# A one-row output stored as four pieces from two queues, in a decode kernel with grouped attention and two MLP steps

## The chip, the cores and the metric

The kernel runs on 1 core of one Trainium2 chip. The metric is device time in microseconds (us), the median of several runs. Beside it stands one profiled execution, whose trace gives the start and duration of every instruction. The engines are TensorE (PE; its weight loads PEld), VectorE (DVE), ScalarE (ACT), GpSimd (POOL) and SyncE (SP). A name with a q (SPq, ACTq) is the engine's instruction queue, which also issues transfers (DMAs).

## What is computed

One token of 512 numbers goes through a layer norm, an attention over a cache of 16,384 positions with 32 query heads on 8 key/value heads, and a second block. With a sequence of one, all four shifted groups of that block are zero, so that only its layer norm and the two-layer MLP are left.

```
x = A_x                                                   # (1, 1, 512) bf16
h = x + _A_ref(_layernorm(x), A_k_cache, A_v_cache, A_wq, A_wo)
h2 = h + _B_ref(_layernorm(h), B_w1, B_w2, B_w3, B_w4)
...
def _A_ref(x, k_cache, v_cache, wq, wo):
    q = heads(x @ wq)
    scores = einsum("bhqd,bhkd->bhqk", q, repeat(k)) * Dh ** -0.5
    o = einsum("bhqk,bhkd->bhqd", softmax(scores), repeat(v))
    return merge(o) @ wo
def _B_ref(x, w1, w2, w3, w4):
    hs = concatenate(shifted groups of gelu(layernorm(x) @ w1)) @ w2
    x1 = x + hs
    return x1 + gelu(layernorm(x1) @ w3) @ w4
```

The output is one row of 512 bf16 numbers, 1 KB.

## The kernel before

The caches and weights, some 79 MB, are streamed from device memory by SyncE through the helper `load` (its DMA is L216). For each of the 8 key/value heads, VectorE transposes the keys (`kt`, L390), TensorE makes scores (L399), ScalarE exponentiates (L425), TensorE transposes the weights and multiplies by the values (L455), and the results are gathered (L467). Keys are held in a ring of two buffers `kb`, values in a ring of three `vb`; the last loads are the output projection `wo` and the MLP weights w3 and w4, w4 in four pieces. ScalarE issues a single load, the input `x4` (four rows of 128 numbers), at the start.

The end of the program goes: the projection with `wo` (L533), the row's mean and variance, the product with w3 (L546), gelu on ScalarE (L558), a transpose on VectorE (L562), the product with w4 (L567), and the sum on VectorE into `fin` (L571). `fin` is a tile of 128 partitions by 128 numbers. TensorE worked with each column copied 32 times, so partitions 0, 32, 64 and 96 hold the four quarters of the output and the other partitions hold copies. The store (L573) takes these four partitions, 256 B each, and writes them to the four quarters of `out`.

The order on each engine is that in which the code records the operations: `Program.op` keeps a list per engine, works out which earlier operations each one depends on, and `emit` turns these into semaphore waits ahead of the instruction. Every DMA has a semaphore of its own name, which is raised by 16 when the whole transfer has landed. The last operation, a `nop` on SyncE that reads the output, makes SyncE wait for the landing; in the built program that wait stands on the branch that leaves the block (L146). Behind it come a drain on each engine and a barrier over all of them, and the program ends.

Of the kernel before, what the change touches and what calls it, by code (L numbers as in the profile page):

```python
# [131 lines left out]
def bass_sequential_preLN__gqa_block_cached__mixer_s_mlp__decode_kernel(  # L132
# [13 lines left out]
    with ExitStack() as ctx:  # L146
        sb = lambda name, shape, dt: ctx.enter_context(nc.sbuf_tensor(name, shape, dt))
        ps = lambda name, shape, dt: ctx.enter_context(nc.psum_tensor(name, shape, dt))
        P = Program(nc, ctx)
# [49 lines left out]
        fin = sb("fin", [128, 128], BF16)  # L199
# [48 lines left out]
        def piece(cuts, m):  # L248
            return [lo <= m < hi for lo, hi in cuts].index(True)
# [71 lines left out]
        for b in range(2):  # L321
            for e_ in range(2):
                n = 2 * b + e_
                P.op("POOL", lambda e, n=n, b=b, e_=e_: e.affine_select(
                    out=selq_f[:, n, :], in_=selq_f[:, n, :], pattern=[[-2, 32]], compare_op=ALU.not_equal,
# [5 lines left out]
            r=["ident"], w=["quarter"])  # L331
# [8 lines left out]
            r=["hT", (("st", 0), 0), (("st", 0), 6)], w=["xn"])  # L340
# [3 lines left out]
            r=["selq_f"], w=["selq"])  # L344
        dve(lambda e: e.memset(nscale[:, :], -SCALE), w=["nscale"])
        act(lambda e: e.activation(scr[0:1, 0:1], mean4[0:1, 0:1], ACTF.Exp), r=["mean4"], w=["scr"])
        for i in range(2):
# [5 lines left out]
            r=["ident_f"], w=["row32"])  # L353
        dve(lambda e: e.tensor_reduce(row4[:, :], row32[:, :].rearrange("p (a u h) -> p u h a", a=4, u=2)[:, 0, :, :], AX.X, ALU.add),
            r=["row32"], w=["row4"])
        dve(lambda e: e.tensor_reduce(maskdd[:, :], ident_f[:, :].rearrange("p (n d) -> p d n", d=4), AX.X, ALU.add),
            r=["ident_f"], w=["maskdd"])
# [3 lines left out]
            r=["row32"], w=["zo"])  # L361
# [4 lines left out]
        for h in range(HQ):  # L366
            for k in range(NCH):
# [3 lines left out]
                   r=["xn"] + [("wo", n) for n in range(len(WO))], w=["n"], bank=["mn"])  # L371
# [100 lines left out]
        for g in range(HKV + 1):  # L472
# [33 lines left out]
            if g == HKV - 1:  # L506
# [7 lines left out]
                for n, (lo, hi) in enumerate(W4):  # L514
                    load(f"w4{n}", w4_sb[:, lo:hi, :], w4_in[:, lo:hi, :], ("k", 1, 2 + n))
                act(lambda e: e.activation(scr[0:1, 1:2], mean4[0:1, 0:1], ACTF.Gelu_apprx_tanh),
                    r=["mean4"], w=["scr"])
# [8 lines left out]
            r=["o_m"], w=["o_f"])  # L526
# [3 lines left out]
           r=["quarter", "x4"], w=[("O", 0)], bank=[("O", 0)])  # L530
        for r_ in range(32):
            for q in range(4):
# [3 lines left out]
                   r=["o_b", ("wo", piece(WO, r_))], w=[("O", 0)], bank=[("O", 0)])  # L536
# [4 lines left out]
            r=["hT", (S, 0)], w=["hc"])  # L541


        for k in range(NCH):
            for q in range(4):
                pe(lambda e, k=k, q=q: e.matmul(s_ps[32 * q:32 * q + 32, 0, 0:FQ], hc[:, k, :],  # L546
                                                w3_sb[:, k, q * FQ:(q + 1) * FQ], start=(k == 0), stop=(k == NCH - 1)),
                   r=["hc", ("k", 1, piece(W3, k))], w=[("s", 0)], bank=[("s", 0)])
# [5 lines left out]
            r=["hr", (S, 0), (S, 6)], w=["xs"])  # L554
# [10 lines left out]
        for m in range(NHC):  # L565
            for o in range(4):
# [3 lines left out]
                   r=[("hcol", 2 * m // NHC), ("k", 1, 2 + piece(W4, m))], w=["n"], bank=["mn"])  # L570
        dve(lambda e: e.tensor_tensor(fin[:, :], xsum[:, :], n_ps[:, 0:128], ALU.add),  # L571
            r=["n", "xsum"], w=["fin"], bank=["mn"])
        P.op("SP", lambda e: e.dma_start(out[0, 0:1, :].rearrange("o (q j) -> (o q) j", q=4), fin[0:128:32, :]),  # L573
             r=["fin"], w=["out"], dma="out")
        P.op("SP", lambda e: e.nop(), r=["out"])
        P.emit()

    return nc
# [28 lines left out]
```

## Time and profile before

| | us |
|---|---|
| median of 3 runs | 193.95 (193.80 to 193.97) |
| the profiled execution | 194.09 |
| its span, first to last instruction | 192.3 |
| VectorE busy in it | 120.1 |
| TensorE busy in it | 112.8 |
| ScalarE busy in it | 16.9 |

The DMA engines move 79.32 MB at a mean of 413 GB/s, and their busy share is nine tenths or more in 38 of the 40 slices of the span; the first slice has six tenths and the last one. The profiled execution's time is 1.8 us longer than its span: what lies before the first and behind the last recorded instruction.

Times in the views are in us from the span's start unless marked ns. A row of the timeline has the start, the duration, the engine, the line, the operation and its tiles; an x and a number say how many instructions were merged. A DMA's row on a queue is the time for which the engine was occupied with issuing it, not the transfer. In the list of waits a row names who waited, for whom, the total, how often and the longest. In the listing of one line's instructions, the three numbers are the shortest, median and longest duration in ns.

### The profile page before, as it was taken

What the parts mean: (1) busy time and instruction counts of PE and PEld (TensorE: products, weight loads), DVE (VectorE), ACT (ScalarE), POOL (GpSimd) and SP (SyncE); (2) the same over time, 40 slices, a digit from 0 to 9 for tenths busy, and PEclk for the clock granted to TensorE, in tenths of its full rate; (3) what the DMA queues carried; (4) which work ended last, traced back from release to release, by engine and by line L of the source; (5) the groups of instructions that cost most, each with busy time, mean ns of one, the idle gap of its engine ahead of it and who ended that gap; (6) DMA issues with size and microseconds to landing.
All of it is one profiled execution on the core that took longest, in us unless ns stands there. A gap on an engine that the chain in (4) does not pass through costs nothing.

```text
span 192.3 us, 2626 instructions
## 1 busy us (share of the span) xinstructions
PE 112.8 (59%) x1106; PEld 55.9 (29%) x1106; DVE 120.1 (62%) x225; ACT 16.9 (9%) x38; POOL 6.6 (3%) x26
## 2 busy tenths in 40 slices
PE   1025045658837766774686558645785676595443
PEld 1025001242234235223422432233223422454311
DVE  4844099499349929964795369546953796303170
ACT  3000000030030030003000300030003000600010
POOL 2000000000000000000000000000000000000060
PEclk9999999999985695588559655975558559669555
DMA  6999999999999999999999999999999999999991
GB/s 232 436 429 429 433 436 426 436 441 433 406 426 464 429 392 426 477 433 392 423 447 419 429 416 433 443 433 416 447 445 412 402 429 423 426 418 421 417 376 48
DMA packets 5066, 79.32 MB, mean 413 GB/s; under 512 B 576, under 2 KB 576, under 8 KB 1344
## 3 DMA queue, kind: packets, MB, share of 16 engines
q1 hardware_dynamic: 5048, 79.17, 96.9%
q8 instruction: 8, 0.13, 0.3%
q14 instruction: 2, 0.02, 0.0%
q10 hardware_dynamic: 8, 0.00, 0.0%
HBM read 79.17 MB, written 0.00 MB: 412 GB/s over the span
## 4 chain that ended last, share of the span: by engine, by line
DMA 40%; DVE 14%; SPq 5%; issue 2%; PE 1%
DMA kb<-in_A_k_cache_dram 30%; DVE kt L390 13%; DMA kb<-in_B_w_dram 10%; SPq L216 5%; DVE mx L407 1%; PE T_ps L435 0%; DVE pt L441 0%; PE mn_ps L567 0%; DVE fin L571 0%; PE A_ps L446 0%; SPq L102 0%; DVE o_sb L464 0%
## 5 line engine op out<-in xcount | busy, mean ns | idle before, releaser
L390 DVE STREAM_TRANSPOSE kt<-kb 128x1024 int32<-128x1024 int32 x64 | 74.0, 1212 | 11.2 <-DMA kb<-in_A_k_cache_dram 11.1
L399 PE MATMUL s_ps<-kt,qb 128*32 128x512 bf16 x256 | 47.5, 556 | 32.3 <-DVE kt L390 32.3
L455 PE MATMUL O_ps<-vb,pt 128*16 128x512 bf16 x224 | 28.9, 529 | 0.0
L399 PEld LDWEIGHTS s_ps<-kt,qb 128*32 128x32 bf16 x256 | 10.6, 113 | 61.9 <-DVE kt L390 54.1
L425 ACT ACTIVATE p_sb<-s_ps,bias 128x512 bf16<-128x512 f32 x16 | 12.8, 824 | 150.1 <-PE mn_ps L419 114.1
L467 PE MATMUL A_ps<-o_sb,zo 128*128 128x128 f32 x64 | 15.7, 422 | 10.3 <-DVE o_sb L464 10.3
L441 DVE COPY pt<-T_ps 64x256 bf16<-64x256 bf16 (+2 forms) x40 | 9.8, 261 | 15.6 <-PE T_ps L435 15.2
L407 DVE TENSOR_REDUCE mx<-s_ps 128x1 f32<-128x512 f32 x16 | 10.8, 677 | 11.9 <-PE s_ps L399 9.9
L435 PE MATMUL T_ps<-ident,p_sb 128*128 128x128 bf16 x128 | 11.8, 250 | 10.9 <-ACT p_sb L425 10.9
L467 PEld LDWEIGHTS A_ps<-o_sb,zo 128*128 128x128 f32 x64 | 13.4, 310 | 11.4 <-DVE o_sb L464 11.4
L435 PEld LDWEIGHTS T_ps<-ident,p_sb 128*128 128x128 bf16 x128 | 8.9, 112 | 12.9 <-ACT p_sb L425 12.7
L455 PEld LDWEIGHTS O_ps<-vb,pt 128*16 128x16 bf16 x224 | 9.4, 114 | 9.8 <-issue 8.5
L368 PE MATMUL mn_ps<-xn,wqo 128*128 128x1 bf16 x128 | 3.6, 165 | 9.1 <-DMA wqo<-in_A_wq_dram 9.1
L412 PE MATMUL mn_ps<-ident_f,mx 128*1 128x128 f32 x32 | 7.3, 323 | 2.5 <-DVE mx L407 2.5
L464 DVE COPY o_sb<-O_ps 128x512 f32<-128x512 f32 x8 | 5.5, 691 | 4.9 <-PE O_ps L455 4.6
L431 POOL COPY p_sb<-p_sb 128x64 bf16<-128x64 bf16 x8 | 1.9, 236 | 160.7 <-ACT p_sb L425 160.7
L368 PEld LDWEIGHTS mn_ps<-xn,wqo 128*128 128x128 bf16 x128 | 3.5, 104 | 9.2 <-issue 9.2
L415 DVE TENSOR_REDUCE nm<-mn_ps 1x4 f32<-1x256 f32 x8 | 3.2, 406 | 3.7 <-PE mn_ps L412 3.7
L533 PE MATMUL O_ps<-wqo,o_b 128*32 128x128 bf16 x128 | 3.0, 253 | 3.0 <-DMA wqo<-in_A_wo_dram 1.7
L412 PEld LDWEIGHTS mn_ps<-ident_f,mx 128*1 128x1 f32 x32 | 2.3, 90 | 7.7 <-DVE mx L407 5.4
L419 PEld LDWEIGHTS mn_ps<-nm,nscale 1*128 1x128 f32 x16 | 2.5, 198 | 5.5 <-DVE nm L415 5.5
L258 DVE TENSOR_SCALAR_CACHE_REDUCE hr<-O_ps 128x128 f32<-128x128 f32 x2 | 0.6, 292 | 5.5 <-PE O_ps L533 4.8
(79 smaller groups left out, 55.9 us busy)
## 6 DMA issues: line engine op xcount, KB each, us to landing
kb<-in_A_k_cache_dram SPq DMA_DIRECT2D x8, 4096.0 KB, 26.7
vb<-in_A_v_cache_dram SPq DMA_DIRECT2D x14, 2048.0 KB, 24.4
wqo<-in_A_wq_dram SPq DMA_DIRECT2D x1, 4096.0 KB, 12.4
kb<-in_A_v_cache_dram SPq DMA_DIRECT2D x2, 2048.0 KB, 26.6
wqo<-in_A_wo_dram SPq DMA_DIRECT2D x2, 1280.0 KB, 32.8
kb<-in_B_w_dram SPq DMA_DIRECT2D x1, 1344.0 KB, 22.9
wqo<-in_A_wo_dram SPq DMA_DIRECT2D x1, 1024.0 KB, 36.2
kb<-in_B_w_dram SPq DMA_DIRECT2D x1, 640.0 KB, 24.8
```

The lines of the kernel that those rows point to most:

```text
L216: P.op(by, lambda e: e.dma_start(dst, src), w=[key, *also], dma=name)
L368: pe(lambda e, h=h, k=k: e.matmul(n_ps[:, h:h + 1], wqo[:, k * HQ * DH + h * DH:k * HQ * DH + (h + 1) * DH], xn[:, k:k + 1], start=(k == 0 ...
L390: dve(lambda e, i=i, view=view: e.transpose(view(kt), view(kb[i])), r=[("k", i, n) for n in range(KPARTS)], w=[("kt", t)])
L399: pe(lambda e, g=g, half=half, n=n, ct=ct, c8=c8: e.matmul(s_ps[32 * ct:32 * ct + 32, half, :], qb[:, n, g, :, :, :].rearrange("p a u h -> ...
L407: dve(lambda e: e.tensor_reduce(mx[:, half:half + 1], s_ps[:, half, :], AX.X, ALU.max), r=[("s", half)], w=[("mx", half)], bank=[("s", half)])
L412: pe(lambda e, half=half: e.matmul(m_ps[0:1, half * 128:half * 128 + 128], mx[:, half:half + 1], ident_f[:, :], start=True, stop=True), r= ...
L425: act(lambda e, half=half, g=g: e.activation(p_sb[:, half * 512:half * 512 + 512].rearrange("p (l s x) -> p l x s", l=8, x=2), s_ps[:, hal ...
L435: pe(lambda e, w=w: e.transpose(T_ps[:, w, :], p_sb[:, w * 64:w * 64 + 128], ident[:, :]), r=[("p", w // 8), ("p", (w + 1) // 8), "ident"] ...
L441: dve(lambda e, lo=lo, w0=w0, w1=w1, l0=l0: e.tensor_copy(to[lo:lo + 64, l0:l0 + w1 - w0, :, :], of[lo:lo + 64, w0:w1, :, lo // 64, 0, :]) ...
L455: pe(lambda e, q=q, ct=ct, n=n: e.matmul(O_ps[g % 2][32 * ct:32 * ct + 16, :], pt[g % 2][:, ct, A, 4 * q:4 * q + 4, :].rearrange("p l h -> ...
L464: dve(lambda e, g=g: e.tensor_copy(o_sb[g % 2][:, :], O_ps[g % 2][:, :]), r=[("O", g % 2)], w=[("osb", g % 2)], bank=[("O", g % 2)])
L467: pe(lambda e, g=g, j=j: e.matmul(A_ps[:, 0:128], zo[:, j, 112 - 16 * g:240 - 16 * g], o_sb[g % 2][:, j * 128:(j + 1) * 128], start=False, ...
```

## The change

The one store of four rows on SyncE becomes four stores of one row each: quarters 0 and 2 are issued by SyncE, 1 and 3 by ScalarE. Each has a semaphore of its own (`out0` to `out3`), and the last operation on SyncE waits for all four. The instruction order of TensorE, VectorE and GpSimd is unchanged.

```
-        P.op("SP", lambda e: e.dma_start(out[0, 0:1, :].rearrange("o (q j) -> (o q) j", q=4), fin[0:128:32, :]),
-             r=["fin"], w=["out"], dma="out")
-        P.op("SP", lambda e: e.nop(), r=["out"])
+        for q in range(4):
+            P.op(("SP", "ACT")[q % 2], lambda e, q=q: e.dma_start(out[0, 0:1, q * 128:(q + 1) * 128],
+                                                                  fin[32 * q:32 * q + 1, :]),
+                 r=["fin"], w=[("out", q)], dma=f"out{q}")
+        P.op("SP", lambda e: e.nop(), r=[("out", q) for q in range(4)])
```

## The prediction

> **What bounds the kernel now.** I read the chain of waits first, cut to its last 32 us. The columns are start, duration, what:
>
> ```profile
> 169.90 0.04 issue
> 169.94 19.49 DMA kb<-in_B_w_dram
> 189.43 0.04 issue
> 189.48 0.43 PE mn_ps L567 x5
> 189.91 0.02 issue
> 189.94 0.29 DVE fin L571
> ```
>
> The kernel streams weights and caches until 189.43 us: the last piece of w4 lands, the last matmuls of L567 run for 0.43 us, and VectorE writes `fin` in 0.29 us. The chain view stops there, but the program does not. What follows comes from the timeline of the last microseconds, then from the waits of SyncE's queue, then from the listing of the instructions of L146 (the end of the block):
>
> ```profile
> 190.25 0.63 SPq L573 DMA_DIRECT2D out_dram<-fin  x1
> ```
>
> ```profile
> SPq L146 <- DMA out_dram<-fin: 1.0, 1, 1.0
> ```
>
> ```profile
> L146 SPq COMPARE_BRANCH x1: 33/33/33, 191.9 to 191.9; - x1
> L146 SPq DRAIN x1: 7/7/7, 192.1 to 192.1; - x1
> ```
>
> So the store sits naked at the end. It is issued for 0.63 us (190.25 to 190.88), SyncE waits 1.0 us more for the landing (about 191.9), then branches, drains and passes the closing barrier until the span ends at 192.3. Nothing else runs: the other engines stand in that barrier. A microsecond added before the landing is a microsecond of span. The change touches only this stretch.
>
> **The change, part by part.** It removes one issue on SyncE of 0.63 us. It adds two issues on SyncE, one behind the other, and two on ScalarE, one behind the other, all four released by the same `fin`. SyncE then waits for four semaphores, not one. Nothing is moved past other work: behind each queue stands only the closing barrier, and the order of PE, DVE and POOL is the same.
>
> *What one issue costs* is not in the trace for a single-row store, so I bound it by the rows for other issues. The listing of L216 (the helper `load`) gives minimum, median and maximum in ns, and the chain gives the pattern inside one batch of loads:
>
> ```profile
> L216 SPq DMA_DIRECT2D vb<-in_A_v_cache_dram x14: 327/328/531, 2.1 to 140.0; - x14
> L216 ACTq DMA_DIRECT2D x<-in_A_x_dram x1: 553/553/553, 0.7 to 0.7; - x1
> L216 SPq DMA_DIRECT2D wqo<-in_A_wq_dram x1: 391/391/391, 0.7 to 0.7; - x1
> ```
>
> ```profile
> 160.93 0.33 SPq L216
> 161.26 0.04 issue
> 161.30 0.43 SPq L216
> 161.73 0.04 issue
> ```
>
> A load of 128 rows takes SyncE 0.33 us when it comes alone and 0.43 us right behind another, with 0.04 us between. The only store takes 0.63 us. ScalarE has one issue in the whole trace: `x4`, 4 rows of 256 B, 0.55 us.
>
> On SyncE, two issues therefore take between 0.33 + 0.04 + 0.43 = 0.80 us (priced as loads) and 0.63 + 0.04 + 0.63 = 1.30 us (priced as the store), or 1.40 us if the second pays the 0.10 us that loads pay back to back. Against 0.63 us this is +0.17 to +0.77.
>
> On ScalarE the nearest row is `x4`: same engine, rows of the same size. Two of these take 0.55 + 0.04 + 0.55 = 1.14 us, or +0.51 against 0.63 us. The low bound is the load price on SyncE (+0.17); the high one is 0.63 + 0.04 + 0.73 = 1.40 us, or +0.77.
>
> The two engines work side by side, so the later pair counts. By their nearest rows that is ScalarE's, unless SyncE's pair is priced wholly as the store. I take +0.51. What it is covered by: nothing, since `fin` is the last computation. ScalarE itself is free in time: its last activation (L558) starts at 185.93 and takes 0.85 us for its two pieces.
>
> *From the end of an issue to the landing* I keep the 1.0 us of the old store for each new one. It cancels. Its bounds: four landings at once could be slower by what I can't price except by queueing (below); a smaller one could be quicker. The windows view (window, length, busy time of five engines, clock, DMA share, GB/s) shows when bytes moved, for the store and for the first loads:
>
> ```profile
> 191.20:191.40 0.20, 0.00 (x0) 0.00 (x0) 0.00 (x0) 0.00 (x0) 0.00 (x0) 0.50 0.00 0
> 191.40:191.60 0.20, 0.00 (x0) 0.00 (x0) 0.00 (x0) 0.00 (x0) 0.00 (x0) 0.50 0.03 5
> ```
>
> ```profile
> 1.40:1.60 0.20, 0.00 (x0) 0.00 (x0) 0.00 (x0) 0.20 (x1) 0.20 (x1) 1.00 0.00 0
> 1.60:1.80 0.20, 0.00 (x0) 0.00 (x0) 0.11 (x1) 0.20 (x1) 0.20 (x2) 1.00 3.05 823
> ```
>
> The store's bytes move in 191.4 to 191.6, at least 0.52 us after its issue ended at 190.88. After the `x4` issue, which ended at 1.26, the first bytes come in 1.6 to 1.8, as early as 0.34 us. So a new store could gain about 0.2 us here (0.52 - 0.34 = 0.18): the low bound of this term is -0.2, the high one 0.
>
> The Trainium skill, in DMA: Bandwidth & Descriptors, section "Latency and other measured facts", puts most of the fixed cost of a small DMA into the receipt of the write at its target. By that rule four stores in flight would share one receipt and the extra issues would hardly matter (the second rival, below). The trace agrees in part only: of 1.65 us from issue to landing at least 1.15 us are over before the first byte moves, and at most 0.5 us (191.4 to 191.9) is left for the receipt.
>
> *The waits.* In the changed program SyncE waits first for `out3` (ScalarE's second), then in one instruction for `out1` and `out2`, and the closing branch waits for `out0`. Before, the branch alone waited. A wait that is already satisfied has this price in the listing of L102:
>
> ```profile
> L102 SPq EVENT_SEMAPHORE x19: 17/17/17, 33.8 to 160.9; - x19
> ```
>
> With about 0.03 us of issue beside it (as in the chain at 160.90) that is 0.05 us each. `out3` lands last by the sum above, so the two steps behind it lie on the path: +0.10. If SyncE's store were last, one step follows: +0.05.
>
> *Sum:* +0.51 + 0.10 = +0.61 us. Bounds: the low one is the load price, quicker first bytes and one wait, 0.17 - 0.2 + 0.05 = about 0; the high one without queueing between the engines is 0.77 + 0.10 = +0.87. The profiled execution took 194.09 us (span 192.3, the rest around it, which the change does not touch), so it would become 194.70. The median of the runs shown is 193.95, 0.14 us less; the same step gives 194.56, which I forecast.
>
> **The rivals.** The bound between same and different is 0.2%, 0.39 us, about what a measurement of this kernel tells from no change: faster is below 193.56, slower above 194.34.
>
> 1. *All single rows issue like loads, on both engines.* Then the pair costs +0.17 and the waits +0.10: +0.27, 194.22, within the bound. For it: 0.33 us is the commonest price on SyncE, and the store's 0.63 may come from its step over four partitions 32 apart, which a single row lacks. Against it: ScalarE's only issue shows 0.55, and it is a plain load.
>
> 2. *Not slower: a store of one row starts its bytes sooner, by what the second issue costs.* Load prices (+0.17), first bytes 0.2 us sooner after the issue, as after `x4` (-0.2), and one wait (+0.05): +0.02, 193.97. It decides when the time from the end of the second issue to the landing falls below 1.0 - 0.17 - 0.05 = 0.78 us. For it: the 0.34 us to first bytes after `x4`. Against it: `x4` is a load from another engine, and its window holds the bytes of `wq` too. A gain above 0.39 us would need the old 0.63 us issue to shrink more than two new ones add, and no row shows an issue under 0.327 us, so two exceed it.
>
> 3. *The two engines queue for one another.* If the four issues run in series, the last ends after 4 x 0.43 + 3 x 0.04 = 1.84 us, +1.21, and with one wait +1.26: 195.21. Priced as the store they would take 4 x 0.63 + 0.12 = 2.64 us, +2.01 and 196.0. Against it speaks the start of the span: ScalarE's `x4` and SyncE's `wq` are issued together (0.71 and 0.72 us), and `wq` takes 0.39 us, only 0.06 above the 0.33 alone. For it: `x4` itself took 0.55, and how much of that was waiting can't be seen. The Trainium skill, in Perfetto Trace Analysis, section "DMA Instruction — HWDGE (DVE, Sync)", says that the block that generates descriptors is locked by one issuer at a time, and that the wait for the lock is counted in the instruction's duration. By that rule full series would give the 195.21 above; the 0.06 us of `wq` shows little of it here.
>
> **How the numbers follow.** The forecast has 0.54: each step has a row of the right engine or kind. Rival 1 has 0.17, since it needs a price on ScalarE that no row shows. Rival 2 has 0.10, needing two favourable bounds together. Rival 3 has 0.16: one overlap speaks against it, but four issues in a microsecond were never seen. The remaining 0.03 is a drift of the whole program below 193.56 with no mechanism. Slower: 0.52 of the forecast (0.02 is for its lower edge under 194.34) and 0.16, together 0.68. Same: 0.17 + 0.02 and 0.08 of rival 2, 0.27. Faster: 0.02 of rival 2 by drift and 0.03, 0.05. The range runs from 194.0 (rival 2's time, half of it left out) to 195.2 (rival 3 with load prices; the part above it left out). The forecast's own range is 194.3 (+0.51 - 0.2 + 0.05) to 194.8 (+0.87).
>
> **What would show it.** In the changed profile the two SPq rows and the two ACTq rows should start near 190.25. If ScalarE's rows are 0.55 us or more and end after SyncE's, and SyncE's longest wait at the end names ScalarE's second store, the forecast's path is right. Rows of 0.33 and 0.43 on both engines mean rival 1 or 2; the window in which the last bytes move then decides: bytes less than 0.4 us after the last issue mean rival 2. Rows on one engine that grow while the other's run, to a sum above 1.4 us, mean rival 3. The distance from the last landing to the span's end is 0.4 us now and should be 0.1 more. The packets also tell how a row is cut: the page counts 576 packets under 512 B, and 35 loads of 16 small packets plus 8 each for `x4` and the store make 576. With one data packet a row it stays 576. The prediction is wrong if the stretch before 190.25 changes by more than the forecast itself, or if the last issue ends before 191.05.

## The result and the profile after

The changed kernel takes 194.29 us in the median of 20 runs (194.09 to 194.68), the kernel before 194.04 in 20 runs beside it (193.80 to 194.27). The ratio is 1.0015, with a 95% interval of 1.0009 to 1.0021; by the medians it is 0.25 us slower. That is a loss clear of the noise, but inside the bound of 0.2% that the prediction called the same. The forecast was +0.61 us.

The end of the timeline after the change (start, duration, engine, line, operation, tiles, number merged):

```profile
190.02 0.29 DVE L571 TENSOR_TENSOR fin<-xsum,mn_ps 128x128 bf16<-128x128 f32 x1 [2.10 <-PE mn_ps L567]
190.34 0.62 SPq L574 DMA_DIRECT2D out_dram<-fin  x2
190.34 0.55 ACTq L574 DMA_DIRECT2D out_dram<-fin  x2
```

Two single-row stores take SyncE 0.62 us and ScalarE 0.55 us, where the one store of four rows took 0.63. The listing of L574 separates them (shortest, median, longest, in ns):

```profile
L574 SPq DMA_DIRECT2D out_dram<-fin x2: 254/288/323, 190.3 to 190.7; - x2
L574 ACTq DMA_DIRECT2D out_dram<-fin x2: 248/259/270, 190.3 to 190.6; - x2
```

A single row is issued in 0.25 to 0.32 us. In the trace the second row is the shorter one on SyncE (0.25 after 0.32) and 0.02 us longer on ScalarE (0.27 after 0.25). The bytes move in two groups (windows view: window, length, five engines, clock, DMA share, GB/s):

```profile
191.00:191.10 0.10, 0.00 (x0) 0.00 (x0) 0.00 (x0) 0.00 (x0) 0.00 (x0) 0.50 0.03 5
191.10:191.30 0.20, 0.00 (x0) 0.00 (x0) 0.00 (x0) 0.00 (x0) 0.00 (x0) 0.50 0.00 0
191.30:191.40 0.10, 0.00 (x0) 0.00 (x0) 0.00 (x0) 0.00 (x0) 0.00 (x0) 0.50 0.02 3
191.40:191.50 0.10, 0.00 (x0) 0.00 (x0) 0.00 (x0) 0.00 (x0) 0.00 (x0) 0.50 0.01 3
```

The first stores' bytes go in 191.0 to 191.1, the second stores' in 191.3 to 191.5. Measured from the end of `fin` (190.31 here, 190.22 before), the last bytes leave within 1.2 us, and before the change they left at 1.2 to 1.4. Then come the waits, in the list of SyncE's queue and the listings of L577 (the closing `nop`) and L146:

```profile
SPq L102 <- DMA out_dram<-fin: 0.8, 1, 0.8
```

```profile
L577 SPq EVENT_SEMAPHORE  x1: 130/130/130, 191.8 to 191.8; - x1
```

```profile
L146 SPq COMPARE_BRANCH  x1: 33/33/33, 192.0 to 192.0; - x1
```

SyncE waits 0.8 us for `out3`, then 0.13 us more in the wait for `out1` and `out2`: its own second store lands last, not ScalarE's. From the end of `fin` to the start of the closing branch, to the nanosecond in the trace, it takes 1.71 us, against 1.68 before. The part of the program that the change touches became 0.03 us longer.

So where do 0.25 us come from? Each run has both its device time and its span. Their difference, the time around the span, shows where they lie: it is 1.80 us on average in the 29 runs of the kernel before that were taken beside the first experiments (1.75 to 1.87) and 2.03 in the 20 runs of the changed one (1.92 to 2.09). The spans of single runs are on record to 0.1 us, so the averages are what counts. The mean span is 192.24 before and 192.28 after. Most of the loss lies outside the recorded instructions, where the prediction had put nothing. The page still counts 576 packets under 512 B, so each row went as one data packet. The experiments look for what moved the time around the span, and for what an issue's price hangs on.

The table holds what they gave. "ScalarE" is the number of instructions more than in the kernel before (built program, without waits). "Tail" is the time from the end of `fin` to the start of SyncE's closing branch in the profiled execution. "Around" is the mean over the runs of device time minus span. Times are medians, the kernel before in its own batch beside them. All in us.

| kernel | ScalarE | tail | around | time | before |
|---|---|---|---|---|---|
| before | 0 | 1.68 | 1.80 | | 194.04 |
| changed | +2 | 1.71 | 2.03 | 194.29 | 194.04 |
| e1_one_sem | +2 | 1.65 | 2.00 | 194.15 | 194.05 |
| e2_all_sp | 0 | 2.18 | 1.80 | 194.56 | 194.05 |
| e3_four_act | +1 | 1.70 | 1.81 | 193.94 | 194.05 |
| e4_adjacent | 0 | 1.22 | 1.80 | 193.60 | 194.05 |
| e5_two_acts | +2 | 1.67 | 2.02 | 194.14 | 194.05 |
| e6_all_act | +4 | 2.16 | 2.00 | 194.57 | 194.05 |
| e7_pairs | +1 | 1.31 | 1.81 | 193.68 | 194.05 |
| e8_x4_three | +2 | 1.67 | 2.02 | 194.25 | 194.05 |
| e9_after_one_gelu | +1 | 1.72 | 1.82 | 194.03 | 193.98 |
| e10_before_one_gelu | -1 | 1.67 | 1.81 | 194.00 | 193.98 |
| e11_pairs_one_sem | +1 | 1.32 | 1.80 | 193.68 | 193.98 |
| e12_step2 | 0 | 1.77 | 1.81 | 194.10 | 193.98 |

### The profile page after: what moved, and what is told of

Same layout as the page of the kernel before. It is cut to its first block, busy times and chain, and to the rows that moved or that the text cites. A ratio compares the mean times of both kernels' runs of the same rounds, so it can differ in the third digit from the quotient of the medians.

```text
span 192.4 us, 2631 instructions
## 1 busy us (share of the span) xinstructions
PE 112.3 (58%) x1106; PEld 56.2 (29%) x1106; DVE 120.1 (62%) x225; ACT 16.9 (9%) x38; POOL 6.6 (3%) x26
## 4 chain that ended last, share of the span: by engine, by line
DMA 40%; DVE 14%; SPq 5%; issue 2%; PE 1%
DMA kb<-in_A_k_cache_dram 30%; DVE kt L390 13%; DMA kb<-in_B_w_dram 10%; SPq L216 5%; DVE mx L407 1%; PE T_ps L435 0%; DVE pt L441 0%; PE mn_ps L567 0%; DVE fin L571 0%; DVE o_sb L464 0%; PE A_ps L446 0%; SPq L102 0%
## 5 line engine op out<-in xcount | busy, mean ns | idle before, releaser
L455 PE MATMUL O_ps<-vb,pt 128*16 128x512 bf16 x224 | 28.3, 516 | 0.0
L533 PE MATMUL O_ps<-wqo,o_b 128*32 128x128 bf16 x128 | 3.5, 305 | 1.3 <-DVE o_b L527 1.3
L419 PE MATMUL mn_ps<-nm,nscale 1*128 1x4 f32 x16 | 3.2, 270 | 1.3 <-DVE nm L415 0.9
```

The lines of the kernel that those rows point to most:

```text
L419: pe(lambda e: e.matmul(n_ps[:, 0:REP], nscale[0:1, :], nm[0:1, :], start=True, stop=True), r=["nm", "nscale"], w=["n"], bank=["mn"])
L455: pe(lambda e, q=q, ct=ct, n=n: e.matmul(O_ps[g % 2][32 * ct:32 * ct + 16, :], pt[g % 2][:, ct, A, 4 * q:4 * q + 4, :].rearrange("p l h -> ...
```

## The experiments

**One semaphore (e1).** The changed kernel, with the four stores raising one semaphore:

```
-                 r=["fin"], w=[("out", q)], dma=f"out{q}")
+                 r=["fin"], w=[("out", q)], dma="out")
```

> The changed kernel with one semaphore for the four stores, so that the closing branch alone waits (for 64). Theory A (the small loss lies at the end of the program: the last landing plus the two extra wait steps): the two SPq and two ACTq rows stay at 0.62 and 0.55 us in sum, the stretch from the last store row's end to the branch shrinks by about 0.07 us, and the time falls from +0.25 to about +0.15 to +0.2 us against the kernel before. Theory B (the loss hangs on the number of semaphores or on what lies outside the span): the time returns to within 0.05 us of the kernel before. Theory C (the loss hangs on ScalarE issuing at the end): the time stays at +0.25 us.

Measured: 194.15 against 194.05, ratio 1.0009 (1.0000 to 1.0018). The tail shrinks by 0.06 us to 1.65, less than before the change: three semaphores more cost the two extra steps behind the last landing and, as far as these runs show, nothing else. The time around the span stays at 2.00. So theory B falls in its first half (the number of semaphores), and what is left of the loss is neither the landings nor the waits.

**All four on one engine (e2, e6).** The changed kernel with one name in place of the alternation:

```
-            P.op(("SP", "ACT")[q % 2], lambda e, q=q: e.dma_start(out[0, 0:1, q * 128:(q + 1) * 128],
+            P.op("SP", lambda e, q=q: e.dma_start(out[0, 0:1, q * 128:(q + 1) * 128],
```

and "ACT" in place of "SP" in e6.

> All four single rows issued by SyncE, with four semaphores. Theory A: rows of 0.25 to 0.32 us with 0.04 between make about 1.2 us of issue in place of 0.63, so the time is 0.5 to 0.6 us above the kernel before. Theory C (ScalarE at the end costs 0.2 us by itself): only 0.3 to 0.4 us above. If single rows were issued at the price of the old store (0.63 us each), it would be about 2.0 us above.

> All four single rows issued by ScalarE. Inside the span, from the end of fin to SyncE's closing branch, about 2.15 to 2.2 us as with all four on SyncE (2.18), 0.5 more than before. Theory E (the 0.2 us outside the span come with the number of DMAs that ScalarE issues, three or more, its load included): time minus span 2.0 and time about 0.7 us above the kernel before. Theory F (they come when both queues carry the output's stores): time minus span 1.80 and time 0.5 us above.

Measured: 194.56 with SyncE alone, ratio 1.0026 (1.0016 to 1.0036); 194.57 with ScalarE alone, 1.0032 (1.0020 to 1.0044). Both tails are about 0.5 us longer than before, as reckoned from rows of 0.25 us. The listings of L574 in e2 and in e6:

```profile
L574 SPq DMA_DIRECT2D out_dram<-fin x4: 246/254/312, 190.3 to 191.3; - x4
```

```profile
L574 ACTq DMA_DIRECT2D out_dram<-fin x4: 240/274/275, 190.1 to 191.0; - x4
```

Alone on its engine a row is issued in the same time as beside the other engine's rows, so the two engines don't queue for one another in issuing. The time around the span is 1.80 with SyncE alone, which issues three DMAs more and waits twice more than before, and 2.00 with ScalarE alone. Theory F (both queues at once) falls with that. The time of e6 fits less well: tail and time around the span add up to +0.68 us, and its six runs give +0.52 by the medians and +0.62 by the ratio.

**The four-row store on ScalarE (e3).** The kernel before, one name changed:

```
-        P.op("SP", lambda e: e.dma_start(out[0, 0:1, :].rearrange("o (q j) -> (o q) j", q=4), fin[0:128:32, :]),
+        P.op("ACT", lambda e: e.dma_start(out[0, 0:1, :].rearrange("o (q j) -> (o q) j", q=4), fin[0:128:32, :]),
```

> The old store of four rows, issued by ScalarE in place of SyncE; SyncE still waits for it. Theory A: one ACTq row of 0.55 to 0.65 us, time within 0.1 us of the kernel before. Theory C (ScalarE at the end costs something outside the span): 0.2 us or more above the kernel before with the same tail inside the span.

Measured: 193.94 against 194.05, ratio 0.9996 (0.9987 to 1.0004), around the span 1.81. A late store on ScalarE alone costs nothing, against theory C. Its row:

```profile
190.06 0.61 ACTq L573 DMA_DIRECT2D out_dram<-fin  x1
```

So the 0.6 us belong to this store, not to SyncE.

**ScalarE's instructions counted (e5, e8, e9, e10).** e5 adds two tiny activations at the start of the kernel before; e8 cuts its load `x4` into three DMAs, for which the two matmuls that read it then wait (not shown):

```
+        for n in (2, 3):
+            act(lambda e, n=n: e.activation(scr[0:1, n:n + 1], mean4[0:1, 0:1], ACTF.Exp), r=["mean4"], w=[("scr", n)])
```

```
-        load("x4", x4[:, :], A_x[0, 0:1, :].rearrange("o (q j) -> (o q) j", q=4), "x4", "ACT")
+        for n, (lo, hi) in enumerate(((0, 2), (2, 3), (3, 4))):
+            load(f"x4{n}", x4[lo:hi, :], A_x[0, 0:1, :].rearrange("o (q j) -> (o q) j", q=4)[lo:hi, :], ("x4", n), "ACT")
```

> The kernel before with two more one-element activations on ScalarE at its start (they write scratch that nothing reads), so that ScalarE has as many instructions as in the changed kernel, without its late stores. So far time minus span is 1.80 us in every kernel but the changed one and its one-semaphore form, where it is 2.0. Theory D (that 0.2 us hangs on the number of ScalarE's instructions): time minus span 2.0, time 0.2 us above the kernel before. Theories E and F (below): 1.80, and the time within 0.1 us of the kernel before.

> The kernel before with its small load x4 cut into three DMAs on ScalarE (two rows, one, one) at the start, so that ScalarE issues three DMAs in all and none at the end. The start is covered by the load of wq, for which TensorE waits 9 us. Theory E: time minus span 2.0, time 0.2 us above the kernel before. Theory F: 1.80, within 0.1 us.

Measured: around the span 2.02 in both. The times are 194.14 for e5, ratio 1.0010 (1.0000 to 1.0020), and 194.25 for e8, 1.0013 (1.0004 to 1.0023). e5 has no DMA more than the kernel before, and its end is that of the kernel before:

```profile
189.96 0.29 DVE L573 TENSOR_TENSOR fin<-xsum,mn_ps 128x128 bf16<-128x128 f32 x1 [2.08 <-PE mn_ps L569]
190.27 0.62 SPq L575 DMA_DIRECT2D out_dram<-fin  x1
```

The intervals of e1 and e5 start at 1.0000, so their times alone don't show the loss; the time around the span does. e5 rules theory E out as well: two activations at 2.7 us do what two stores at 190 us did. Theory D (the number of ScalarE's instructions) is left, and e9 tests it on the changed kernel itself. It merges the two halves of the last gelu, which takes one instruction away from ScalarE; e10 does the same to the kernel before:

```
-        for n in range(2):
-            lo, hi = n * NHC // 2, (n + 1) * NHC // 2
-            act(lambda e, lo=lo, hi=hi: e.activation(
...
+        act(lambda e: e.activation(
+            hg[:, :], s_ps[:, 0, 0:FQ], ACTF.Gelu_apprx_tanh, scale=s[:, 7:8]),
+            r=[("s", 0), (S, 7)], w=[("hg", 0), ("hg", 1)], bank=[("s", 0)])
+        for n in range(2):
+            lo, hi = n * NHC // 2, (n + 1) * NHC // 2
```

> The changed kernel with the last gelu as one activation over 448 columns in place of two over 224, so that ScalarE has one instruction less, that is one more than in the kernel before. The transposes and matmuls behind the gelu start some 0.4 us later, but the last piece of w4 lands 1.9 us behind them, so the end should not move. Theory D (time minus span goes from 1.80 to 2.02 us with the second additional instruction on ScalarE): time minus span 1.80, time about 0.22 us below the changed kernel, 194.05 to 194.1. If the 0.2 us hang on the late stores after all: time minus span 2.0, time 194.3.

> The kernel before with the same single gelu: the control for the run above. Time minus span 1.80 and time within 0.1 us of the kernel before; if the later transposes do reach the end, the span grows and the same amount has to be taken off the run above.

Measured: e9 194.03 against 193.98, ratio 0.9999 (0.9991 to 1.0008), around the span 1.82; e10 194.00, ratio 0.9999 (0.9990 to 1.0008), around the span 1.81. The four stores are as in the changed kernel, and the loss is gone:

```profile
190.26 0.61 SPq L573 DMA_DIRECT2D out_dram<-fin  x2
190.27 0.55 ACTq L573 DMA_DIRECT2D out_dram<-fin  x2
```

In every kernel with 0 or 1 more instructions on ScalarE, or one less, the time around the span is 1.80 to 1.82 on average; with 2 or 4 more it is 2.00 to 2.03. The single runs of the two groups don't meet: they lie at 1.74 to 1.88 and at 1.90 to 2.10. It is a step of 0.2 us, not a price for each.

**What makes the old store's issue long (e4, e12).** Both are the kernel before with other partitions read:

```
-        ... fin[0:128:32, :]),
+        ... fin[0:4, :]),
```

and `fin[0:8:2, :]` in e12. All four rows that they store hold the first quarter of the output; the other three quarters are left out.

> The old store, with its four rows read from partitions 0 to 3 in place of 0, 32, 64, 96: all four rows stored are then copies of the first quarter of the output. If the old store's 0.63 us come from its step over partitions, the row falls to 0.25 to 0.35 us and the time to 0.3 to 0.5 us below the kernel before. If they come from four rows or from storing as such, the row stays at 0.6 and the time within 0.1 us of the kernel before.

> The old store with its four rows read from partitions 0, 2, 4 and 6: all four rows stored are copies of the first quarter of the output. If any step other than to the next partition makes the issue long, the row is 0.6 us as before and the time within 0.1 us of the kernel before. If only the step of 32 (into other groups of partitions) does, the row is 0.35 us and the time 0.45 us below, as with partitions 0 to 3.

Measured: e4 193.60, ratio 0.9975 (0.9965 to 0.9985); e12 194.10, ratio 1.0006 (0.9997 to 1.0015). The rows of L573 in e4 and in e12:

```profile
L573 SPq DMA_DIRECT2D out_dram<-fin x1: 348/348/348, 190.1 to 190.1; - x1
```

```profile
L573 SPq DMA_DIRECT2D out_dram<-fin x1: 733/733/733, 190.2 to 190.2; - x1
```

Four neighbouring partitions are issued in 0.35 us; with a step of two it takes 0.73, longer even than with a step of 32. The number of rows, and that it is a store, are not what costs: the step between partitions is. In e4 the landing also comes 0.17 us sooner behind the issue, so that the whole tail is 0.46 us shorter.

**Two pairs of neighbours (e7, e11).** Each group of 32 partitions holds copies of its quarter, so partitions 31 and 32 hold quarters 0 and 1, and 95 and 96 hold quarters 2 and 3. In place of the old store and its `nop` stand:

```
+        for n in range(2):
+            P.op(("SP", "ACT")[n], lambda e, n=n: e.dma_start(
+                out[0, 0:1, n * 256:(n + 1) * 256].rearrange("o (q j) -> (o q) j", q=2),
+                fin[64 * n + 31:64 * n + 33, :]), r=["fin"], w=[("out", n)], dma=f"out{n}")
+        P.op("SP", lambda e: e.nop(), r=[("out", n) for n in range(2)])
```

> Two stores of two rows each, one from SyncE and one from ScalarE, that take the rows from neighbouring partitions (31 and 32, 95 and 96; every partition of a group of 32 holds a copy of its quarter, so the output is whole). Issue rows as for the adjacent store (0.35 us) and about 1.25 us from the end of fin to the closing branch against 1.68 before: 0.4 us less inside the span. Theory E: time minus span 1.80, time 0.4 us below the kernel before. Theory F: time minus span 2.0, time 0.2 us below. If the cheap row needs all its partitions from 0 up, the rows stay at 0.6 and the time is not below.

> The two stores of two neighbouring rows once more (the same program as e7_pairs), to narrow its interval: issue rows of 0.25 to 0.32 us, about 1.3 us from the end of fin to the closing branch, time minus span 1.80, time 0.35 to 0.45 us below the kernel before.

(e11 is the same program as e7, despite its label.) Measured: 193.68 in both, ratio 0.9983 (0.9974 to 0.9992) and 0.9982 (0.9973 to 0.9991). Both queues carry the output's stores, and the time around the span is 1.81 and 1.80, against theory F once more. The rows of e7:

```profile
190.28 0.32 SPq L574 DMA_DIRECT2D out_dram<-fin  x1
190.29 0.25 ACTq L574 DMA_DIRECT2D out_dram<-fin  x1
```

One cheap issue on each engine, side by side, and one instruction more on ScalarE, which stays below the step. This version is faster than both kernels, by some 0.35 us against the one before, with the whole output.

## Why the prediction was right or wrong

*The bound, and where the change acts:* right. The store stands naked behind `fin`, and the experiments that moved the tail clearly changed the time by as much where the time around the span stayed at 1.80: +0.50 in e2 (time +0.51), -0.46 in e4 (time -0.45), -0.37 in e7 (time -0.37).

*The direction:* right, but not for the reason given. A loss this small is what the prediction called the same; it gave that 0.27, and slower 0.68.

*The issue pair, "I take +0.51":* the term that was mis-sized. ScalarE's pair measured 0.55 us in all in place of 1.14, and SyncE's 0.62, so the term is about 0 (0.62 - 0.63). The prediction had itself named a last issue that ends before 191.05 as a sign that it is wrong: the last one ended at 190.96, and it was SyncE's, not ScalarE's. Two rows misled. `x4` at 0.55 us was taken as the price of a small transfer on ScalarE, where the runs show 0.24 to 0.28 for each single row. What the row of `x4` does price can be seen in e8, where `x4` goes in three pieces:

```profile
L216 ACTq DMA_DIRECT2D x<-in_A_x_dram x3: 234/269/548, 0.7 to 1.6; - x3
```

In the trace the first piece, two rows, takes the 0.55 us, and the single rows behind it 0.23 and 0.27; two rows took ScalarE 0.25 in e7. So 0.55 is what ScalarE's first issue takes at the start of the program, with two rows as with four; why is not shown. And the 0.10 us that loads pay back to back is not paid: the second row is the shorter one on SyncE. The reason given for rival 1, that the old store's price comes from its step over partitions, is what e4 and e12 show; a single row has no such step. Rival 1 still put the pair too high (+0.17).

*The landing, "It cancels":* right in size, by two things that offset each other. From the end of SyncE's last issue to the last landing it took 1.0 us, as before. First bytes came 0.4 to 0.5 us behind an issue's end where the old store took 0.6, the direction of rival 2, but on SyncE the rest took longer and used the gain up. The traces show when: with one queue alone, in e2 and e6, each row lands 0.77 to 0.83 us behind the end of its issue. With both queues ScalarE's two rows take 0.83 and 0.88 us, but SyncE's 0.94 and 1.00, and in e7 SyncE's pair takes 0.95. So SyncE's landings are some 0.15 us later when ScalarE's stores run beside them; no run shows why. The receipt rule cited from the Trainium skill (DMA: Bandwidth & Descriptors, section "Latency and other measured facts") does not carry this case: from a store's first byte to its landing there are 0.35 to 0.5 us of a tail of 1.7. In e4 the issue alone is 0.29 us shorter, of the 0.46 by which the tail shrank.

*The waits, +0.10:* 0.06 was measured, and the order was another. `out3` was to land last; SyncE's own second store did, 0.18 us later. For that order the prediction had +0.05. e1 takes the extra steps away and gains 0.06 us in the tail.

*Rival 3, the engines queueing:* no sign of it in the issues. The lock rule from the Trainium skill (Perfetto Trace Analysis, section "DMA Instruction — HWDGE (DVE, Sync)") would lengthen rows that overlap; the rows with two engines (0.25 to 0.32 us) are those of e2 and e6 with one (0.24 to 0.31).

*"the rest around it, which the change does not touch":* this is the step that failed in kind. The rest around the span grew by 0.22 us, 0.25 less the tail's 0.03, and e9 returns it by taking a gelu instruction out. The prediction took this time as fixed without a reason and had no rival for it: its sum saw only the path through recorded instructions. So the measured +0.25 us is not a smaller version of the forecast's +0.61, and near rival 1's +0.27 by chance alone. The size of the whole was inside the range because an overestimate in the tail stood where another cost appeared.

What stays open is why the time around the span has this step. The trace also holds semaphores that are raised outside the span. In the five kernels with the step, those in the last 0.4 us ahead of the span and in the 1.9 us behind it come on average within 0.01 us of where they come in the kernel before. So the 0.2 us are no delay of these steps, and the profile doesn't show what took them. The Trainium skill (Runtime: NRT & Kernel Launch, section "Instruction fetch mechanics") says that an engine's program is fetched in blocks of 256 instructions, and calls the cost of crossing into the next block mostly hidden. A block's end between the first and the second added instruction could make a step of this kind, but no run here shows that one lies there. The profile pages of all kernels count the same packets of the kind "instruction" within the span:

```profile
q8 instruction: 8, 0.13, 0.3%
q14 instruction: 2, 0.02, 0.0%
```

SyncE had three stores and two waits more in e2, without a step; the other engines were not tried.

## What to carry to other kernels

The issue of a transfer at the naked end of a program is paid in full, and its price hangs on the pattern: for the stores here 0.25 to 0.35 us for one row or for neighbouring partitions, 0.6 to 0.7 for partitions with a step. ScalarE's first issue of the program, 0.55 us, was no measure for its later ones, 0.24 to 0.28. Where copies of the data let neighbours be chosen, choose them before splitting the transfer. When a change of a few tenths of a microsecond is judged, compare device time minus span as well as the span: here two more instructions on ScalarE, at the start or at the end, cost 0.2 us, and the edit's own stretch grew by 0.03.

## What was unexpected of the hardware

The step around the span: 1.80 to 1.82 us with at most one instruction more on ScalarE, 2.00 to 2.03 with two or four more, in 13 kernels, whether these were loads, stores or activations. The price of a step between partitions: four rows from partitions 0 to 3 took 0.35 us to issue, from 0, 32, 64, 96 0.63, and from 0, 2, 4, 6 0.73. And SyncE's stores landed 0.94 to 1.00 us behind their issue beside ScalarE's stores, 0.77 to 0.82 without.
